# Two more raw tiles by DMA transpose in a mixer and MLP kernel on one core

## The chip, the cores and the metric

The kernel runs on one core of a Trainium2 chip. The metric is the device time of one execution in microseconds (us); the time of a kernel is the median of several runs. The core's engines work side by side and meet at semaphores: TensorE (PE, with its weight loads as PEld) multiplies, VectorE (DVE) makes the statistics, the norms and the sums, ScalarE (ACT) evicts and applies the gelu, GpSimd (POOL) makes the roots, and SyncE (SP) issues nearly all DMAs, in the order of its queue.

## The reference

The input x has 2048 rows of 512, in bf16. What is computed:

```python
h = gelu(layernorm(x) @ w1)                    # w1: 512 x 512
# four column blocks of h, shifted by +1, -1, +2, -2 rows, zeros at the ends
hs = concatenate([g0, g1, g2, g3], axis=-1) @ w2
x1 = x + hs
h2 = gelu(layernorm(x1) @ w3) @ w4             # w3: 512 x 1792, w4: 1792 x 512
return x1 + h2
```

## The kernel before

The rows are cut into 16 tiles of 128 rows; tile t holds the rows 16p + t, so that a shift of the rows by one is the same partition in the next tile, except at the ends. A tile is 128 KB.

The first product, x @ w1, needs each tile with its columns on the partitions (xnT). It is reached in two ways. Tiles 6 to 15 are normed first: statistics (st, L289), their aggregate (ag, L294), the root on POOL (rs, L300), the norm (nm, L309); then they are transposed in pairs, the pairs 8 and 10 on TensorE (tp8, tp10, L323, eight 128x128 transposes each, evicted by ACT as ev8, ev10, L332), the pairs 6, 12 and 14 by a DMA transpose from SBUF (td0_6, td0_12, td0_14, L343). A pair's product is m1p (L410), and ACT writes its gelu (g1p, g1s, L420 and L425) in the transposed layout that the second product wants.

Tiles 0 to 5 are raw: they are transposed as they come from memory, multiplied as they are (m1r, L378), copied out by ACT (rc, L388), and the layernorm is put right afterwards by DVE (zr, L393) with the column sums of w1 (colsum, L366, four matmuls cs0 to cs; their eviction is cse, L370). Tiles 0 to 3 are transposed on TensorE, four transposes each (tp0 to tp3, L323), and evicted by ACT (ev0 to ev3, 128x512). Tiles 4 and 5 come transposed by one DMA straight from DRAM (tdx_4, L351). The raw tiles' gelu (g1r, L399) is transposed by DMA in pairs (th, L357).

Then follow the second product and the sum x1 (m2, L436 and L450; L460 on DVE), the second layernorm with its DMA transposes (td1, L343), and the two big products of the MLP (m3h L492 and m3 L468 with w3, m4 L511 with w4), with their outputs. They begin at tile 8.

The order on each engine is written out by hand in lists of names (firsts, from L634); what is not in a list follows in the order of the code. Every operation waits for what it reads and writes over by semaphores. An engine, and SP with its DMAs, takes its list strictly in order, so an operation that waits holds up all that stand behind it on that engine. Loads are named ldx (a tile of x, L272), ldw1 (L542), ldw2 (L546), ldw3a and ldw3b (L552). Their order on SP before:

```python
firsts["sp"] = """ldx0 ldw11 ldx6 ldw13 ldx7 ldx2 ldx8 ldx3 ldx9 tdx_4 ldx10 ldx11 ldx12 td0_6 ldx13 ldx14 ldx15
    ldw20 ldw21 ldw22 ldw23 td0_12 td0_14 ldw3a0 ldw3a1 ldw3a2 ldw3a3 th_0 td1_8 ldw3b0 ...
```

ACT's queue issues three loads at the start (ldw10, ldw12, ldx1).

Of the kernel before, what the change touches and what calls it, by code (L numbers as in the profile page):

```python
# [171 lines left out]
def bass_standalone__mixer_s_mlp__prompt_kernel(nc: bass.Bass, x, w1, w2, w3, w4, out):  # L172
# [15 lines left out]
    with ExitStack() as es:  # L188
# [82 lines left out]
        def load_x(t, n, eng="sp"):  # L271
            add(eng, f"ldx{t}", lambda e: e.dma_start(x_sb[:, t : t + n, :], xd[:, t : t + n, :]),  # L272
                writes=[(("x", i), 0) for i in range(t, t + n)], dma=True)
# [40 lines left out]
        def tp(t, n, b, raw):  # L314
            src = x_sb if raw else xn
            rd = [(("x", i), 0) if raw else (("xn", i), 0) for i in range(t, t + n)]

            def f(e):
                ins = None
                for i in range(n):  # L320
                    for c in range(DC):
                        o = 1024 * b + (i * DC + c) * P
                        ins = e.transpose(psb[:, o : o + P], src[:, t + i, P * c : P * (c + 1)], ident[:])  # L323
                return ins

            add("pe", f"tp{t}", f, reads=rd + [("ident", 1)], writes=bres(b, 1, f"tp{t}"))

        def ev(t, n, b, eng="act"):
            src = psb[:, 1024 * b : 1024 * b + n * D]
            dst = xnT[:, t : t + n, :, :].rearrange("p t c s -> p (t c s)")  # L330
            if eng == "act":
                f = lambda e: e.activation(dst, src, ACT_F.Copy)  # L332
            else:
                f = lambda e: e.tensor_copy(dst, src)
            add(eng, f"ev{t}", f, reads=bres(b, 1, f"tp{t}"), writes=[(("xT", i), 0) for i in range(t, t + n)])
# [13 lines left out]
        def tdma_x(t):  # L349
            add("sp", f"tdx_{t}",  # L350
                lambda e: e.dma_start(xnT[:, t : t + 2, :, :].rearrange("p t c s -> p (t c) s"),  # L351
                                      xd[:, t : t + 2, :].rearrange("p t d -> p (t d)"), transpose=True),
                writes=[(("xT", i), 0) for i in (t, t + 1)], dma=True)
# [20 lines left out]
        def m1r(t, b, c0=0, c1=DC):  # L374
            def f(e):
                ins = None
                for c in range(c0, c1):
                    ins = e.matmul(bank(b), xnT[:, t, c, :], w1_sb[:, c, :], start=(c == 0), stop=(c == DC - 1))  # L378
                return ins

            rd = [(("xT", t), 0)] + W1[c0:c1]
            if c0:
                rd += bres(b, 1, f"m1r{t}{c0}")
            end = f"{c1}" if c1 < DC else ""
            add("pe", f"m1r{t}{end}", f, reads=rd, writes=bres(b, 1, f"m1r{t}{end}"))

        def rc(t, b):
            add("act", f"rc{t}", lambda e: e.activation(yraw[:, t, :], bank(b), ACT_F.Copy),  # L388
                reads=bres(b, 1, f"m1r{t}"), writes=[(("yraw", t), 0)])
# [168 lines left out]
        load_w1(2, "act")  # L558
        load_w1(3, "sp")
        load_x(1, 1, "act")  # L560
        for t, n in ((6, 1), (7, 1), (2, 1), (8, 1), (3, 1), (9, 1), (10, 1), (11, 1), (12, 1), (13, 1), (14, 1), (15, 1), (4, 2)):
            load_x(t, n)
        for c in range(DC):
            load_w2(c)
# [7 lines left out]
            colsum(4, c)  # L572
        colsum_out(4)
        for t in range(R):
            if t < 4:
                tp(t, 1, 6 + t % 2, True)
                ev(t, 1, 6 + t % 2, "act")
            elif t == 4:
                tdma_x(t)
            cuts = [0, 1, 2, 3, 4] if t == 0 else [0, 2, 4] if t == 1 else [0, 4]  # L580
            for c0, c1 in zip(cuts, cuts[1:]):
                m1r(t, YB[t], c0, c1)
            rc(t, YB[t])
# [39 lines left out]
        for t in (8, 10):  # L623
# [7 lines left out]
            tdma(1, t, 2)  # L631

        firsts = {}
        firsts["pe"] = """wu tp0 cs0 cs1 m1r01 m1r02 tp1 m1r03 cs2 m1r0 cs tp2 m1r12 m1r1 tp3 m1r2 m1r3 m1r4 m1r5 tp8 m1p6  # L634
            tp10 m1p8 m1p10 m2_8a m2_9a m2_8 m2_9b m2_9 m2_10a m2_11a m2_12a m2_13a m1p12 m1p14 m2_10 m2_11
            m2_12b m2_13b m2_14a m2_15a m2_12 m2_13 m2_14b m2_15b m2_14 m2_15""".split()
        firsts["act"] = """ldw10 ldw12 ldx1 table ev0 ev1 rc0 ev2 ev3 rc1 rc2 rc3 rc4 rc5 ev8 cse g1p6 ev10 g1p8 g1s10 g1s11
            g1r0 g1r1 g1p12 g1p14 g2h_0_0_0 g2h_0_0_4 g1r2 g1r3 g2h_0_0_8 g2h_0_0_12 g1r4 g1r5""".split()
        firsts["dve"] = """pada padb padc padd pade padf st0_0 st0_6 st0_7 ag0_6 ag0_7
            st0_8 nm0_6 nm0_7 st0_9 ag0_8 ag0_9 st0_10 st0_11 nm0_8 nm0_9 ag0_10 ag0_11  # L640
            st0_12 nm0_10 nm0_11 st0_13 ag0_12 ag0_13 st0_14 st0_15 ag0_14 ag0_15 nm0_12 nm0_13 st0_1 ag0_0 ag0_1
            nm0_14 nm0_15 zr0 zr1 x1_8 x1_9 st1_8 st1_9 ag1_8 ag1_9 st0_2 nm1_8 nm1_9 st0_3 ag0_2 ag0_3 x1_10 x1_11 st1_10
            st1_11 ag1_10 ag1_11 x1_12 nm1_10 nm1_11 x1_13 x1_14 x1_15 zr2 zr3 st0_4 st0_5 ag0_4 ag0_5 zr4 zr5
            st1_12 st1_13 ag1_12 ag1_13""".split()
        firsts["pool"] = """ident0 ident1 neghalf stz ste rs0_6 rs0_8 rs0_10
            rs0_12 rs0_14 rs0_0 rs1_8 rs0_2 rs1_10""".split()
        firsts["sp"] = """ldx0 ldw11 ldx6 ldw13 ldx7 ldx2 ldx8 ldx3 ldx9 tdx_4 ldx10 ldx11 ldx12 td0_6 ldx13 ldx14 ldx15 ldw20 ldw21 ldw22 ldw23 td0_12 td0_14 ldw3a0 ldw3a1
            ldw3a2 ldw3a3 th_0 td1_8 ldw3b0 ldw3b1 ldw3b2 ldw3b3 ldx4 td1_10 th_2 th_4 td1_12 td1_14 ldw4""".split()

        slots = [4, 0, 2]  # L650
# [111 lines left out]
```

## Time and profile before

| | before |
|---|---|
| median of 3 runs | 136.77 us (136.63 to 137.22) |
| the profiled execution | 136.71 us, of which the span 134.7 us |
| busy: PE, PEld | 131.6 us (98%), 69.7 us |
| busy: DVE, ACT, POOL | 58.2 us, 46.7 us, 12.5 us |
| granted TensorE clock | 1.0 |
| DMA moved | 12.96 MB, HBM read 6.82 MB |

The span runs from the first to the last instruction. Starts in the timeline are us from the span's start. A row of the timeline has the start, the length, the engine (SPq is a DMA's issue on SP, not its transfer), the line in the code, the operation, what it writes and reads, how many were merged, and in brackets how long the engine was idle before it and what ended that. A DMA lands when its last completion has come.

### The profile page before, as it was taken

Reading aid. Unit: us, or ns where it says so; the run is one execution under the profiler, and the core shown is the slowest. Engines: PE = TensorE matmul, PEld = TensorE weight load, DVE = VectorE, ACT = ScalarE, POOL = GpSimd, SP = SyncE. Lnnn points to the kernel's source line nnn. Section 1 sums busy time; section 2 is a strip of 40 time slices with the busy share of each in tenths; the row PEclk is TensorE's granted clock in tenths of the full one; section 3 lists DMA queues with packets and bytes.
Section 4 is the critical chain, followed back from the end, with each engine's and each line's share of the span. In section 5 each row is a group of like instructions: output and inputs, shape, how many; then the busy total and the mean of one; then the engine's idle time right before and its main releaser. Section 6 shows DMA issues by size and latency. Waiting matters only on the chain.

```text
span 134.7 us, 1809 instructions
## 1 busy us (share of the span) xinstructions
PE 131.6 (98%) x729; PEld 69.7 (52%) x729; DVE 58.2 (43%) x135; ACT 46.7 (35%) x56; POOL 12.5 (9%) x25
## 2 busy tenths in 40 slices
PE   7999999999999999999999999999999999999993
PEld 2446867668884444444444444444444444444452
DVE  0689989799967777762222000122200002322222
ACT  3387871507963035550001555200066630000000
POOL 2032422220330012220000000000000000000000
PEclk9999999999999999999999999999999999999999
DMA  3999489984465893444111000011110001111121
GB/s 110 335 230 198 145 160 246 243 276 95 78 124 101 260 298 75 81 80 78 39 61 56 5 0 0 0 39 39 39 39 5 0 0 39 39 39 39 42 76 43
DMA packets 24568, 12.96 MB, mean 96 GB/s; under 512 B 16752, under 2 KB 23920, under 8 KB 24560
## 3 DMA queue, kind: packets, MB, share of 16 engines
q1 hardware_dynamic: 23984, 12.42, 36.4%
q10 hardware_dynamic: 576, 0.43, 1.0%
q8 instruction: 6, 0.10, 0.3%
q14 instruction: 2, 0.02, 0.1%
HBM read 6.82 MB, written 2.10 MB: 66 GB/s over the span
## 4 chain that ended last, share of the span: by engine, by line
PE 98%; DVE 0%; issue 0%
PE ps L511 36%; PE ps L468 27%; PE ps L492 9%; PE ps L410 6%; PE ps L436 5%; PE ps L450 5%; PE ps L378 4%; PE ps L534 2%; PE ps L323 2%; PE ps L366 1%; DVE o_sb L523 0%
## 5 line engine op out<-in xcount | busy, mean ns | idle before, releaser
L511 PE MATMUL ps<-w_sb,h2T 128*128 128x512 bf16 (+2 forms) x238 | 48.9, 366 | 0.0
L523 DVE TENSOR_TENSOR o_sb<-ps,x_sb 128x512 bf16<-128x512 f32 (+2 forms) x17 | 11.2, 660 | 61.2 <-PE ps L511 61.2
L479 ACT ACTIVATE h2T<-ps 128x1024 bf16<-128x1024 f32 x21 | 21.5, 1024 | 46.2 <-PE ps L468 46.2
L468 PE MATMUL ps<-x1nT,w_sb 128*128 128x512 bf16 x168 | 36.8, 379 | 0.0
L511 PEld LDWEIGHTS ps<-w_sb,h2T 128*128 128x128 bf16 x238 | 22.8, 98 | 25.9
L468 PEld LDWEIGHTS ps<-x1nT,w_sb 128*128 128x128 bf16 x168 | 16.4, 98 | 19.8
L289 DVE BATCH_NORM_STATS2 st<-x_sb 128x6 f32<-128x512 bf16 x32 | 20.9, 681 | 3.9 <-DMA x_sb<-in_x_dram 3.9
L300 POOL TENSOR_TENSOR rstd<-mv,neghalf 128x2 f32<-128x2 f32 x16 | 11.6, 725 | 46.2 <-DVE mv L294 46.2
L492 PE MATMUL ps<-x1nT,w_sb 128*128 128x256 bf16 x112 | 12.4, 273 | 0.0
L460 DVE TENSOR_TENSOR x_sb<-ps,x_sb 128x512 bf16<-128x512 f32 x16 | 10.6, 686 | 2.9 <-PE ps L436 1.5
L492 PEld LDWEIGHTS ps<-x1nT,w_sb 128*128 128x128 bf16 x112 | 10.9, 98 | 1.6
L410 PE MATMUL ps<-xnT,w_sb 128*128 128x256 bf16 x80 | 9.2, 273 | 0.0
L503 ACT ACTIVATE h2T<-ps 128x1024 bf16<-128x1024 f32 (+1 forms) x8 | 7.1, 915 | 6.0 <-PE ps L492 6.0
L410 PEld LDWEIGHTS ps<-xnT,w_sb 128*128 128x128 bf16 x80 | 7.7, 98 | 1.2
L309 DVE TENSOR_SCALAR x1n<-x_sb,mv,rstd 128x512 bf16<-128x512 bf16 x16 | 5.9, 411 | 5.3 <-POOL rstd L300 5.3
L450 PE MATMUL ps<-w_sb,hTf 128*128 128x512 bf16 x32 | 7.2, 379 | 0.0
L436 PE MATMUL ps<-w_sb,hTf 128*128 128x512 bf16 x32 | 7.1, 379 | 0.0
L378 PE MATMUL ps<-w_sb,xnT 128*128 128x512 bf16 x24 | 6.4, 399 | 0.0
L420 ACT ACTIVATE hTf<-ps 128x1024 bf16<-128x1024 f32 x4 | 4.1, 1024 | 4.1 <-PE ps L410 4.1
L332 ACT ACTIVATE xnT<-ps 128x512 bf16<-128x512 bf16 (+1 forms) x6 | 4.4, 736 | 2.6 <-PE ps L323 2.6
L294 DVE BATCH_NORM_AGGREGATE mv<-st 128x2 f32<-128x9 f32 x32 | 5.0, 186 | 0.0
L436 PEld LDWEIGHTS ps<-w_sb,hTf 128*128 128x128 bf16 x32 | 3.1, 98 | 3.6
(28 smaller groups left out, 37.1 us busy)
## 6 DMA issues: line engine op xcount, KB each, us to landing
out_dram<-o_sb SPq DMA_DIRECT2D x15, 128.0 KB, 1.8
w_sb<-in_w_dram SPq DMA_DIRECT2D x1, 1792.0 KB, 8.0
x_sb<-in_x_dram SPq DMA_DIRECT2D x13, 128.0 KB, 3.2
w_sb<-in_w_dram SPq DMA_DIRECT2D x4, 256.0 KB, 4.4
w_sb<-in_w_dram SPq DMA_DIRECT2D x6, 128.0 KB, 3.1
w_sb<-in_w_dram SPq DMA_DIRECT2D x4, 192.0 KB, 3.1
w_sb<-in_w_dram ACTq DMA_DIRECT2D x2, 128.0 KB, 3.3
x_sb<-in_x_dram SPq DMA_DIRECT2D x1, 256.0 KB, 3.9
```

The lines of the kernel that those rows point to most:

```text
L289: add("dve", f"st{layer}_{t}", lambda e: e.bn_stats(st9[:, i, 0:6], src[:, t, :]), reads=[(r, 0)], writes=[(("st6", i), 0)])
L300: lambda e: e.tensor_tensor(rstd[:, i : i + n], mv[:, i : i + n, 1], neghalf[:, 0:n], ALU.pow),
L378: ins = e.matmul(bank(b), xnT[:, t, c, :], w1_sb[:, c, :], start=(c == 0), stop=(c == DC - 1))
L410: ins = e.matmul(dst, w1_sb[:, c, P * fc : P * (fc + 1)], xnT[:, t : t + 2, c, :], start=(c == 0), stop=(c == DC - 1))
L436: ins = e.matmul(bank(b), hTf[:, c0 : c0 + P], w2_sb[:, j, :], start=(j == 0), stop=(j == DC - 1))
L450: ins = e.matmul(bank(b), hTf[:, w[0] : w[0] + P], w2_sb[:, j, :], start=first and n == 0, stop=last and n == len(js) - 1)
L460: lambda e: e.tensor_tensor(x1_sb[:, t, :], bank(b), x_sb[:, t, :], ALU.add),
L468: ins = e.matmul(bank(b), w3_sb[:, c, P * fc : P * (fc + 1)], x1nT[:, 4 * q : 4 * q + 4, c, :], start=(c == 0), stop=(c == DC - 1))
L479: lambda e: e.activation(h2T[:, fc : fc + 2, q % 2, :], src, ACT_F.Gelu_apprx_tanh),
L492: ins = e.matmul(dst, w3_sb[:, c, P * (fc + i) : P * (fc + i + 1)], x1nT[:, t : t + 2, c, :], start=(c == 0), stop=(c == DC - 1))
L511: ins = e.matmul(ps[:, 512 * b : 512 * b + c1 - c0], h2T[:, fc, q % 2, P * i : P * (i + 1)], w4_sb[:, fc, c0:c1], start=(fc == 0), stop=(f ...
L523: lambda e: e.tensor_tensor(o_sb[:, k % 4, c0:c1], ps[:, 512 * b : 512 * b + c1 - c0], x1_sb[:, t, c0:c1], ALU.add),
```

## The change

Tiles 2 and 3 are no longer transposed on TensorE: one DMA transpose from DRAM, tdx_2, brings both, as tdx_4 does for 4 and 5. tp2, tp3, ev2 and ev3 go. The plain loads of x2 and x3, which the later sum and the statistics read, become one load of 256 KB that stands behind td0_14 on SP; ldx4 (tiles 4 and 5) keeps its place. On SP tdx_2 stands behind ldx8, and ldw13 has changed places with ldx7. On ACT the eviction of the column sums, cse, moves from behind ev8 to behind rc1. On DVE pair 8 is normed ahead of tile 11's statistics, pair 12 ahead of tile 15's, and tile 2's statistics come behind pair 8's second norm. POOL's list is unchanged.

```diff
-        for t, n in ((6, 1), (7, 1), (2, 1), (8, 1), (3, 1), (9, 1), ..., (15, 1), (4, 2)):
+        for t, n in ((6, 1), (7, 1), (8, 1), (9, 1), ..., (15, 1), (2, 2), (4, 2)):
             load_x(t, n)
...
-            if t < 4:
+            if t < 2:
                 tp(t, 1, 6 + t % 2, True)
                 ev(t, 1, 6 + t % 2, "act")
-            elif t == 4:
+            elif t % 2 == 0:
                 tdma_x(t)
...
-  pe:  ... m1r0 cs tp2 m1r12 m1r1 tp3 m1r2 m1r3 m1r4 m1r5 tp8 m1p6
+  pe:  ... m1r0 cs m1r12 m1r1 m1r2 m1r3 m1r4 m1r5 tp8 m1p6
-  act: ... ev0 ev1 rc0 ev2 ev3 rc1 rc2 rc3 rc4 rc5 ev8 cse g1p6 ev10 ...
+  act: ... ev0 ev1 rc0 rc1 cse rc2 rc3 rc4 rc5 ev8 g1p6 ev10 ...
-  dve: st0_8 nm0_6 nm0_7 st0_9 ag0_8 ag0_9 st0_10 st0_11 nm0_8 nm0_9 ag0_10 ag0_11
-       st0_12 nm0_10 nm0_11 st0_13 ag0_12 ag0_13 st0_14 st0_15 ag0_14 ag0_15 nm0_12 nm0_13 st0_1 ag0_0 ag0_1
-       nm0_14 nm0_15 zr0 zr1 x1_8 x1_9 st1_8 st1_9 ag1_8 ag1_9 st0_2 nm1_8 nm1_9 st0_3 ag0_2 ag0_3 ...
+  dve: st0_8 nm0_6 nm0_7 st0_9 ag0_8 ag0_9 st0_10 nm0_8 nm0_9 st0_11 ag0_10 ag0_11
+       st0_12 nm0_10 nm0_11 st0_13 ag0_12 ag0_13 st0_14 nm0_12 nm0_13 st0_15 ag0_14 ag0_15 st0_1 ag0_0 ag0_1
+       nm0_14 nm0_15 zr0 zr1 x1_8 x1_9 st1_8 st1_9 ag1_8 ag1_9 nm1_8 nm1_9 st0_2 st0_3 ag0_2 ag0_3 ...
-  sp:  ldx0 ldw11 ldx6 ldw13 ldx7 ldx2 ldx8 ldx3 ldx9 tdx_4 ldx10 ldx11 ldx12 td0_6 ... td0_14 ldw3a0
+  sp:  ldx0 ldw11 ldx6 ldx7 ldw13 ldx8 tdx_2 ldx9 tdx_4 ldx10 ldx11 ldx12 td0_6 ... td0_14 ldx2 ldw3a0
```

More of the change, by code (lines that the diff above doesn't have):

```diff
@@ L560, in bass_standalone__mixer_s_mlp__prompt_kernel @@
         load_x(1, 1, "act")
-        for t, n in ((6, 1), (7, 1), (2, 1), (8, 1), (3, 1), (9, 1), (10, 1), (11, 1), (12, 1), (13, 1), (14, 1), (15, 1), (4, 2)):
+        for t, n in ((6, 1), (7, 1), (8, 1), (9, 1), (10, 1), (11, 1), (12, 1), (13, 1), (14, 1), (15, 1), (2, 2), (4, 2)):
             load_x(t, n)
@@ L633, in bass_standalone__mixer_s_mlp__prompt_kernel @@
         firsts = {}
-        firsts["pe"] = """wu tp0 cs0 cs1 m1r01 m1r02 tp1 m1r03 cs2 m1r0 cs tp2 m1r12 m1r1 tp3 m1r2 m1r3 m1r4 m1r5 tp8 m1p6
+        firsts["pe"] = """wu tp0 cs0 cs1 m1r01 m1r02 tp1 m1r03 cs2 m1r0 cs m1r12 m1r1 m1r2 m1r3 m1r4 m1r5 tp8 m1p6
             tp10 m1p8 m1p10 m2_8a m2_9a m2_8 m2_9b m2_9 m2_10a m2_11a m2_12a m2_13a m1p12 m1p14 m2_10 m2_11
             m2_12b m2_13b m2_14a m2_15a m2_12 m2_13 m2_14b m2_15b m2_14 m2_15""".split()
-        firsts["act"] = """ldw10 ldw12 ldx1 table ev0 ev1 rc0 ev2 ev3 rc1 rc2 rc3 rc4 rc5 ev8 cse g1p6 ev10 g1p8 g1s10 g1s11
+        firsts["act"] = """ldw10 ldw12 ldx1 table ev0 ev1 rc0 rc1 cse rc2 rc3 rc4 rc5 ev8 g1p6 ev10 g1p8 g1s10 g1s11
             g1r0 g1r1 g1p12 g1p14 g2h_0_0_0 g2h_0_0_4 g1r2 g1r3 g2h_0_0_8 g2h_0_0_12 g1r4 g1r5""".split()
         firsts["dve"] = """pada padb padc padd pade padf st0_0 st0_6 st0_7 ag0_6 ag0_7
-            st0_8 nm0_6 nm0_7 st0_9 ag0_8 ag0_9 st0_10 st0_11 nm0_8 nm0_9 ag0_10 ag0_11
-            st0_12 nm0_10 nm0_11 st0_13 ag0_12 ag0_13 st0_14 st0_15 ag0_14 ag0_15 nm0_12 nm0_13 st0_1 ag0_0 ag0_1
-            nm0_14 nm0_15 zr0 zr1 x1_8 x1_9 st1_8 st1_9 ag1_8 ag1_9 st0_2 nm1_8 nm1_9 st0_3 ag0_2 ag0_3 x1_10 x1_11 st1_10
+            st0_8 nm0_6 nm0_7 st0_9 ag0_8 ag0_9 st0_10 nm0_8 nm0_9 st0_11 ag0_10 ag0_11
+            st0_12 nm0_10 nm0_11 st0_13 ag0_12 ag0_13 st0_14 nm0_12 nm0_13 st0_15 ag0_14 ag0_15 st0_1 ag0_0 ag0_1
+            nm0_14 nm0_15 zr0 zr1 x1_8 x1_9 st1_8 st1_9 ag1_8 ag1_9 nm1_8 nm1_9 st0_2 st0_3 ag0_2 ag0_3 x1_10 x1_11 st1_10
             st1_11 ag1_10 ag1_11 x1_12 nm1_10 nm1_11 x1_13 x1_14 x1_15 zr2 zr3 st0_4 st0_5 ag0_4 ag0_5 zr4 zr5
@@ L646, in bass_standalone__mixer_s_mlp__prompt_kernel @@
             rs0_12 rs0_14 rs0_0 rs1_8 rs0_2 rs1_10""".split()
-        firsts["sp"] = """ldx0 ldw11 ldx6 ldw13 ldx7 ldx2 ldx8 ldx3 ldx9 tdx_4 ldx10 ldx11 ldx12 td0_6 ldx13 ldx14 ldx15 ldw20 ldw21 ldw22 ldw23 td0_12 td0_14 ldw3a0 ldw3a1
+        firsts["sp"] = """ldx0 ldw11 ldx6 ldx7 ldw13 ldx8 tdx_2 ldx9 tdx_4 ldx10 ldx11 ldx12 td0_6 ldx13 ldx14 ldx15 ldw20 ldw21 ldw22 ldw23 td0_12 td0_14 ldx2 ldw3a0 ldw3a1
             ldw3a2 ldw3a3 th_0 td1_8 ldw3b0 ldw3b1 ldw3b2 ldw3b3 ldx4 td1_10 th_2 th_4 td1_12 td1_14 ldw4""".split()
```

## The prediction, made before the changed kernel was run

> **What bounds the kernel now.** I read the chain that ended last first, then the same chain in order of time, then the timeline of the first 30 us, and last the busy share of the DMA engines there. The page's busy shares and its chain:
>
> ```profile
> PE   7999999999999999999999999999999999999993
> ...
> DMA  3999489984465893444111000011110001111121
> ...
> PE 98%; DVE 0%; issue 0%
> ```
>
> TensorE is the bound from the first microsecond to the last store, so time is won only where TensorE has less to do, and lost wherever it waits. The DMA row has nines in its second to fourth slices (a slice is 3.37 us, so from 3.4 to 13.5 us): there the transfers are as full as TensorE. The chain in order of time, with start and length in us, around the change:
>
> ```profile
> 7.22 0.22 PE ps L323 x4
> 7.44 0.86 PE ps L378 x4
> 8.31 0.22 PE ps L323 x4
> 8.53 3.45 PE ps L378 x16
> 11.98 0.45 PE ps L323 x8
> 12.43 1.75 PE ps L410 x16
> ```
>
> The two x4 rows of L323 are tp2 and tp3, 0.22 us each, and they are what the change removes. The 16 matmuls of L378 are m1r2 to m1r5; the x8 row is tp8; the L410 row is m1p6, which reads what td0_6 brings. The timeline shows how little time is left there:
>
> ```profile
> 5.01 1.39 SPq L351 DMA_TRANSPOSE xnT<-in_x_dram  x1
> ...
> 8.60 1.26 SPq L343 DMA_TRANSPOSE xnT<-xn  x1
> ...
> 9.64 1.29 DVE L289 BATCH_NORM_STATS2 st<-x_sb 128x6 f32<-128x512 bf16 x2 [0.23 <-DMA x_sb<-in_x_dram]
> ...
> 12.21 1.68 PEld L410 LDWEIGHTS ps<-xnT,w_sb 128*128 128x128 bf16 x16
> ```
>
> DVE waits for tile 10 itself (landed 9.62 by the trace). td0_6 is issued at 8.60 and lands at 12.03, and the weight load of m1p6, which reads it, starts at 12.21: 0.18 us of room. Next, the DMA engines; the last two columns are their busy share and GB/s:
>
> ```profile
> 4.50:5.50 1.00, 1.00 1.06 349
> 5.50:6.50 1.00, 1.00 1.00 305
> 6.50:7.50 1.00, 1.00 1.06 216
> 7.50:8.50 1.00, 1.00 1.15 216
> 8.50:9.50 1.00, 1.00 1.03 286
> 9.50:10.00 0.50, 1.00 0.71 204
> 10.00:11.00 1.00, 1.00 1.21 187
> ```
>
> They are full from 4.5 us until td0_6 lands, but for some 0.15 us after 9.5 (0.29 of half a microsecond). A transfer added ahead of td0_6 therefore delays it. The landings, from the trace's completions: x6 5.12, x1 5.30, w1 row block 3 (ldw13) 5.68, x7 6.06, x2 6.40, x8 6.92, x3 7.28, x9 8.15, tdx_4 9.23, x10 9.62, x11 9.97, x12 10.77, td0_6 12.03.
>
> **The change, part by part.**
>
> *TensorE.* It loses tp2 and tp3: 2 x 0.22 = 0.44 us, all on the path. The floor is thus 136.71 - 0.44 = 136.27 us. The Trainium skill ("TensorE: Matmul & The Clock Gate", Part 4: PE-mode transpose) gives about 275 ns for one such 128x128 transpose in a kernel; its eight would be an estimated 2.2 us, but the trace has 0.22 us for four of them, and the measurement decides.
>
> *DMA work ahead of td0_6.* Two loads (x2, x3) go and one transpose from DRAM (tdx_2) comes. A load: five landings from x1 (5.30) to x3 (7.28) take 1.98 us, 0.40 each. The transpose: x3 (7.28) to x11 (9.97) is 2.69 us for tdx_4 and three loads, so 2.69 - 1.20 = 1.50 us. Added work: 1.50 - 0.79 = 0.71 us, less the 0.15 idle, 0.56. So td0_6 lands at about 12.03 + 0.56 = 12.59. Following the queue gives the same: x8 takes x2's place (6.40), tdx_2 7.90, x9 8.30, tdx_4 9.80, x10 10.2, x11 10.6, and td0_6 2.05 behind it as before (9.97 to 12.03), less the 0.15: 12.5 to 12.65. No row shows two such transposes so close. From below, the second could cost the 1.24 us by which td0_14 lands behind td0_12 (19.47, 20.71); from above, the whole 1.95 us from x3 to tdx_4. I take 1.50, the same operation's own row.
>
> *SP's queue.* Ahead of td0_6 it loses two issues of 0.47 us and gains one transpose issue: 1.39 and a slower next issue (0.57 after tdx_4 instead of 0.43), some 1.55 us. It reaches td0_6 at about 7.97 + 1.55 - 0.95 = 8.57, where before it stood waiting from 7.97 for the norm. The norm of pair 6 comes no later: x7 lands in ldw13's place (5.68 for 6.06), and x8, held up before a transpose as x9 was, at some 6.9, when the statistics of tile 8 started anyway (6.95). So td0_6 is issued at 8.6 as before; only its landing moves. ldw13 lands at 6.06; its first reader's weight load was at 6.41, so nothing there.
>
> *The raw tiles on TensorE.* m1r1's first matmul may start at 7.06; its evicted tile is ready at 6.99, so it starts within 0.1 of that. m1r2 then comes at 7.9 and meets tdx_2 (7.9): 0.1. m1r4 comes at 9.75 and meets tdx_4 (9.80): 0.15 to 0.2. Both waits only use up room that the wait for td0_6 would take anyway: m1r5 ends at 11.65, tp8 runs behind the norm of pair 8 (below), and TensorE stands ready for m1p6 at about 12.15.
>
> *m1p6.* The one weight load that shows a wait for a DMA transpose started 0.10 us after the landing (34.40 to 34.51). So m1p6 loads at 12.59 + 0.10 = 12.69 instead of 12.21, **0.48 us later**. Everything behind is TensorE end to end, so this stays to the end.
>
> *DVE's order.* x10 lands at 10.2 instead of 9.62, statistics 10.2 to 10.9, and now pair 8 is normed before tile 11's statistics: 0.59 behind the start of st0_10, so 10.8 to 11.55; before, 10.85 to 11.57. This move pays for x10's delay and no more. Pair 10 pays instead: tile 11's statistics 0.69, two aggregates 0.3, the root 0.70 with its hand-overs: normed at 13.2 to 13.9 instead of 12.54 to 13.28. tp10 was at 14.01 and now comes at 14.49: covered, but a bound if m1p6 were early. Pair 12 ahead of tile 15: DVE waits 0.2 for its root and td0_12 goes at 16.3 instead of 16.14; m1p12 loads at 21.2, td0_12 lands 3.3 after its issue: hidden. Tile 15 and pair 14 follow: td0_14 goes at 18.7 instead of 17.58 and lands at 21.8; m1p14 starts near 23.6: hidden.
>
> *ACT.* Two evictions fewer (0.60 each) and ncs earlier. Every ACT step behind m1p6 hangs on TensorE (g1p6 waits 0.19, g1p8 0.26), so nothing is won or lost.
>
> *x2-3 behind td0_14.* One 256 KB load, 0.69 us by the spacing of the w3 loads of that size (23.73, 24.48, 25.11), lands near 22.9; the statistics of tile 2 now stand behind pair 8's second norm at 24.1: hidden. But it stands ahead of ldw3a, th_0 and td1_8. th_0 landed 5.43 and td1_8 6.34 us behind td0_14; now 21.8 + 5.43 + 0.69 = 27.9 and 28.85. The matmul that first reads th_0 was at 27.72, now 28.20: covered. The first m3h was at 28.36, now 28.84; with the landing at 28.85 and 0.13 to the first matmul (34.40 to 34.54) it could wait 0.14. Its lower end is no wait (td1_8 is issued at 24.2 and its kind landed in 3.0 to 3.3 elsewhere, 27.5); I take none, since 6.34 holds a stretch (21 to 22.5 us) in which the engines moved little for no reason in this change.
>
> *Sum.* -0.44 of work, +0.92 of waiting: **+0.48 us**. 136.71 (span 134.7 and 2.0 around it) + 0.48 = 137.19; the median of three is 136.77, 0.06 above, so 137.2.
>
> **The rivals.**
>
> *The transpose costs no more than the loads it replaces* (20%). The trace has 1.24 as the least spacing and 1.50 against 0.79, which speaks against it; for it speaks that tdx_4's 1.50 was taken in a mixture. Then td0_6 lands by 12.03, m1p6 is bound by it or by tp10 (x10, issued 0.6 later, lands near 10.0, pair 10 normed by 13.7, 0.25 ahead of before): 0.1 to 0.3 won, 136.5. The Trainium skill ("Advanced Engine Details and Errata", X-Bar Transpose (TRN2)) states that transpose DMAs are as fast as regular ones: by that rule this rival holds. The trace speaks against it: 256 KB in 1.50 us, against 0.79 for two loads.
>
> *The transpose costs more* (20%), the other side. Place: DMA engines between x8 and td0_6. The shift is its cost less 1.02 (0.79 for the loads, 0.15 idle, 0.18 of room less the 0.10 from landing to load); at 1.95 us it is 0.93 and the time 137.6. It counts as slower from 1.76 (137.45). For it: x9, issued before tdx_4, came 0.87 behind x3 and not 0.40.
>
> *td1_8 is late too* (12%): 0.14 more, 137.3; up to 0.5 more if the slow stretch grows.
>
> *The change gives what it removes*, 136.27 (3%): it needs x10 and td0_6 no later than now. The forecast has the remaining 45%.
>
> **How the numbers follow.** A measurement tells about 0.5% (0.68 us) from no change. Faster than that lies below the floor of 136.27: 4%, for errors. Slower is above 137.45: the costly transpose and part of the late td1_8 and of the forecast's upper end: 28%. The rest, 68%, is within. The range runs from the cheap transpose, 136.4, to the costly one with some wait at td1_8, 137.9.
>
> **What would show it.** Right: tdx_2 lands near 7.9, tdx_4 near 9.8, x10 near 10.2, td0_6 near 12.6, and the chain has m1p6's first load near 12.7, with TensorE idle some 0.5 before it. Wrong: td0_6 by 12.1, or TensorE waiting at tp8, tp10, th_0's reader or the first m3h instead.

## The result, and the profile after

The changed kernel takes 137.36 us in the median of 14 runs (136.99 to 137.83), the kernel before 136.73 (136.50 to 137.22): 1.0045 times as long, with a 95% interval of 1.0030 to 1.0059, some 0.6 us. Its profiled execution took 137.14 us, its span is 135.04 us against 134.65.

The time is what the prediction said. The place is not. First the chain that ended last, from the page of the kernel after:

```profile
PE 77%; DVE 9%; DMA 6%; SPq 5%; POOL 2%; issue 1%
```

Before it was TensorE from end to end (98%). Now it runs through loads, DVE's statistics and a DMA before it comes to TensorE. In order of time, the pieces (start, length) around the place where it changes over:

```profile
7.25 2.73 DMA x_sb<-in_x_dram
...
18.05 0.40 DVE xn L309
18.46 1.32 DVE zraw L393 x2
19.78 1.20 DVE x_sb L460 x2
20.98 1.19 DVE st L289 x2
22.17 0.24 DVE mv L294 x2
22.41 0.07 issue
22.48 0.70 POOL rstd L300
23.20 0.73 DVE x1n L309 x2
23.97 4.71 DMA x1nT<-x1n
28.68 0.14 issue
28.81 12.39 PE ps L492 x112
```

The change-over is at 28.68 us, where td1_8 lands and the first m3h may start. Up to there it is DVE's chain and DMAs that set the time; from 28.81 on TensorE runs as before. What TensorE waited for, in the kernel after (total, times, longest):

```profile
PEld ps L378 <- DMA xnT<-in_x_dram: 1.0, 1, 1.0
...
PEld ps L492 <- DVE x_sb L460: 0.7, 1, 0.7
...
PEld ps L450 <- DMA hTf<-hraw: 0.5, 1, 0.5
```

These are idle times of the weight loads, which run ahead of the matmuls; what the matmuls lost is less. The first row is m1r2 waiting for tdx_2: 0.66 us lost from start to start. The third is m2_14 waiting for th_0: 0.19 lost. The second is the first m3h; the row names a sum on DVE, but the semaphore that came last is td1_8's landing: 0.36 lost. The timeline of the kernel after has the first wait, and the issues on SP that stand ahead of the others (the row of 16.11 is two issues, td0_12 and td0_14, with the time between them):

```profile
8.24 3.63 PE L378 MATMUL ps<-w_sb,xnT 128*128 128x512 bf16 x16 [0.49 <-DMA xnT<-in_x_dram]
...
8.82 1.24 SPq L343 DMA_TRANSPOSE xnT<-xn  x1
...
12.15 1.91 PE L410 MATMUL ps<-xnT,w_sb 128*128 128x256 bf16 x16
...
16.11 3.60 SPq L343 DMA_TRANSPOSE xnT<-xn  x2
...
19.76 0.58 SPq L272 DMA_DIRECT2D x_sb<-in_x_dram  x1
...
22.29 1.25 SPq L357 DMA_TRANSPOSE hTf<-hraw  x1
...
23.97 2.70 SPq L343 DMA_TRANSPOSE x1nT<-x1n  x1
...
24.80 3.82 PE L450 MATMUL ps<-w_sb,hTf 128*128 128x512 bf16 x16
```

The two waits behind it stand in a timeline of 17 to 30 us; the matmul's own row of the first m3h names td1_8:

```profile
27.79 0.33 PEld L450 LDWEIGHTS ps<-w_sb,hTf 128*128 128x128 bf16 x3 [0.52 <-DMA hTf<-hraw]
...
28.81 1.36 PE L492 MATMUL ps<-x1nT,w_sb 128*128 128x256 bf16 x11 [0.20 <-DMA x1nT<-x1n]
```

In the kernel before, the first m3h starts without a wait:

```profile
28.36 1.80 PE L492 MATMUL ps<-x1nT,w_sb 128*128 128x256 bf16 x15
```

m1p6 (the L410 row) starts at 12.15, and its first weight load at 12.12 against 12.21 before: the kernel after is 0.11 us **ahead** there in this execution, and still is when the L450 row of 24.80 begins. Both waits that cost time come behind it. Starts of matmuls and landings, read from the traces:

| us | before | after |
|---|---|---|
| tdx_2, tdx_4 land | none, 9.23 | 8.20, 9.55 |
| x10, x11 land | 9.62, 9.97 | 9.98, 10.33 |
| td0_6 issued, lands | 8.60, 12.03 | 8.82, 12.08 |
| m1p6 starts | 12.27 | 12.15 |
| td0_14 issued, lands | 17.58, 20.71 | 18.48, 21.89 |
| th_0 lands, its reader m2_14 starts | 26.14, 27.72 | 27.75, 27.79 |
| td1_8 issued, lands | 23.74, 27.05 | 23.97, 28.68 |
| first m3h starts | 28.36 | 28.81 |

-0.11 at m1p6, +0.19 and +0.36 at the two waits, and -0.06 where before waited for td1_10 (34.40): +0.38 by the traces, and the spans differ by 0.39. The medians differ by 0.63; what makes the rest is in no trace.

### The profile page after: what moved, and what is told of

It reads as the page before. It is cut to its first block, busy times and chain, and to the rows that moved or that the text cites. A ratio compares the mean times of both kernels' runs of the same rounds, so it can differ in the third digit from the quotient of the medians.

```text
span 135.0 us, 1792 instructions
## 1 busy us (share of the span) xinstructions
PE 131.1 (97%) x721; PEld 68.6 (51%) x721; DVE 58.2 (43%) x135; ACT 46.0 (34%) x54; POOL 12.4 (9%) x25
## 4 chain that ended last, share of the span: by engine, by line
PE 77%; DVE 9%; DMA 6%; SPq 5%; POOL 2%; issue 1%
PE ps L511 36%; PE ps L468 27%; PE ps L492 9%; PE ps L436 5%; DMA x1nT<-x1n 3%; DVE st L289 3%; SPq L351 2%; DMA x_sb<-in_x_dram 2%; DVE xn L309 2%; SPq L272 2%; POOL rstd L300 2%; DVE zraw L393 1%; DVE x_sb L460 1%; DVE mv L294 1%; SPq L542 1%
## 5 line engine op out<-in xcount | busy, mean ns | idle before, releaser
L460 DVE TENSOR_TENSOR x_sb<-ps,x_sb 128x512 bf16<-128x512 f32 x16 | 10.6, 682 | 2.0 <-PE ps L436 2.0
L410 PE MATMUL ps<-xnT,w_sb 128*128 128x256 bf16 x80 | 9.2, 273 | 0.0
L410 PEld LDWEIGHTS ps<-xnT,w_sb 128*128 128x128 bf16 x80 | 7.6, 98 | 1.2
L450 PE MATMUL ps<-w_sb,hTf 128*128 128x512 bf16 x32 | 7.4, 380 | 0.0
L436 PEld LDWEIGHTS ps<-w_sb,hTf 128*128 128x128 bf16 x32 | 3.1, 98 | 3.6
L450 PEld LDWEIGHTS ps<-w_sb,hTf 128*128 128x128 bf16 x32 | 3.0, 98 | 3.6 <-DMA hTf<-hraw 0.5
```

Source lines behind the costliest of these rows:

```text
L410: ins = e.matmul(dst, w1_sb[:, c, P * fc : P * (fc + 1)], xnT[:, t : t + 2, c, :], start=(c == 0), stop=(c == DC - 1))
L436: ins = e.matmul(bank(b), hTf[:, c0 : c0 + P], w2_sb[:, j, :], start=(j == 0), stop=(j == DC - 1))
L450: ins = e.matmul(bank(b), hTf[:, w[0] : w[0] + P], w2_sb[:, j, :], start=first and n == 0, stop=last and n == len(js) - 1)
L460: lambda e: e.tensor_tensor(x1_sb[:, t, :], bank(b), x_sb[:, t, :], ALU.add),
```

## The experiments

The theory after the result: th_0 and td1_8 come too late, because td0_14 is issued 0.9 us later and the load of tiles 2 and 3 stands behind it. The rival is the mechanism of the forecast: the loss is made ahead of m1p6 by the second DRAM transpose. A third question is why 0.44 us less work on TensorE gives only 0.11. Ratios are to the kernel before on the same chip, with 95% intervals.

**e5_x2_gap: the load moved to a stretch in which SP is idle.**

```diff
-  sp: ... ldw23 td0_12 td0_14 ldx2 ldw3a0 ...
+  sp: ... ldw23 ldx2 td0_12 td0_14 ldw3a0 ...
```

> The changed kernel with one move: the plain load of tiles 2 and 3 stands behind ldw23, ahead of td0_12, where SP and the DMA engines stand idle (13.6 to 16.1 and 15.7 to 17.0 us in the changed kernel). Theory (late transposes): nothing stands ahead of th_0 and td1_8 that did not before, but td0_14 is still 0.9 us later than before; th_0 lands near 27.0, td1_8 near 28.0, at most 0.1 us of waiting for them and none for ldw3b, 136.6 to 136.8 us. Rival (loss made ahead of m1p6): 137.2 to 137.4.

Measured: 136.80 us, 1.0008 (0.9996 to 1.0019), against 1.0045 with the load behind td0_14. One move of one load takes back most of the loss, and nothing ahead of m1p6 was touched by it; m1p6 even starts later in its trace than in that of the kernel after (12.35 for 12.15). th_0 lands at 26.99 and td1_8 at 27.90, and no matmul waits for either. td0_14 was issued later than in the kernel after (18.98 for 18.48) and td1_8 landed 0.77 earlier all the same, though single landings vary by as much (see e2).

**e2_pair12_old: DVE's order for pair 12 as before, the load where the change put it.**

```diff
-  dve: ... st0_14 nm0_12 nm0_13 st0_15 ag0_14 ag0_15 st0_1 ...
+  dve: ... st0_14 st0_15 ag0_14 ag0_15 nm0_12 nm0_13 st0_1 ...
```

> The changed kernel with before's order for pair 12: tile 15's statistics ahead of its norm. Theory (late transposes): pair 14's norm ends 0.45 us earlier, td0_14 is issued near 18.0 instead of 18.5, th_0 lands near 27.3, td1_8 near 28.2; at most 0.1 us of waiting is left, 136.6 to 136.8 us. If the 256 KB load alone makes the loss: 137.3. Rival (the loss is made ahead of m1p6): 137.2 to 137.4.

Measured: 136.88 us, 1.0012 (0.9996 to 1.0027). This edit alone, too, takes back most. td0_14 was issued at 18.20 instead of 18.48, th_0 landed at 27.02 and td1_8 at 27.95, without a wait. The issue moved by 0.28 us, less than the expected 0.45; the rest of the 0.9 stays, since pair 12 is late already (td0_12 issued at 16.75, 16.14 before). The landing moved by 0.73, which the order does not explain, but one trace does not tell this finely: e6 and e9, described below, have the same program from td0_12 to td1_8 and land td1_8 at 27.87 and 27.08. The medians carry this result, not the trace. That either edit is nearly enough fits a bound with little room: TensorE wants td1_8 some 0.1 ahead of 28.3, and only both together push it past.

**e6_x2_gap_p12: both edits.**

> The same, and before's order for pair 12 as well. Theory (late transposes): td1_8 near 27.6, no wait there; m1p6 starts at 12.1 to 12.3 as in all the kernels so far, so 136.5 to 136.7 us: no more than 0.2 us below before, because the 0.44 us of transposes are spent waiting for tdx_2, tdx_4 and td0_6. Rival (loss made ahead of m1p6): 137.2 to 137.4.

Measured: 136.66 us, 0.9999 (0.9987 to 1.0011): as before, with 0.44 us less to do. m1p6 started at 12.09, the first m3h at 28.27. th_0 landed at 26.93 and td1_8 at 27.87, both in time. td1_8's issue on SP is shorter than above:

```profile
21.66 1.25 SPq L357 DMA_TRANSPOSE hTf<-hraw  x1
...
23.66 2.15 SPq L343 DMA_TRANSPOSE x1nT<-x1n  x1
...
28.27 1.91 PE L492 MATMUL ps<-x1nT,w_sb 128*128 128x256 bf16 x16
```

**e4_before_plus: the kernel before with 512 KB more behind td0_14.**

```diff
+            xdup = sb("xdup", [P, 4, D], BF16)
+            add("sp", "ldxd", lambda e: e.dma_start(xdup[:, 0:4, :], xd[:, 2:6, :]), ...
-  sp: ... td0_14 ldw3a0 ...
+  sp: ... td0_14 ldxd ldw3a0 ...
```

> The kernel before with one DMA more behind td0_14, 512 KB of x into a buffer that nothing reads (twice the load that the change puts there); nothing else is changed. Theory (late transposes): two loads of 0.69 us ahead of th_0 and td1_8 bring them to 27.5 and 28.45; TensorE wants td1_8 by 28.25, so 0.1 to 0.5 us lost, 136.9 to 137.2 us. Rival (the loss is made ahead of m1p6): this stage has room, 136.7 us as before.

Measured: 137.39 us, 1.0043 (1.0028 to 1.0059), above the expected range: the same loss as that of the change, in a kernel that has neither tdx_2 nor the new order on DVE. The profiled execution took 136.83 us (the runs 136.83 to 137.96): td1_8 landed at 28.36 and the first m3h lost 0.19, the only wait behind m1p6. The rest of the median's loss is in no trace. With e5 this points to the place: the stage between td0_14 and the first m3h has room for less than 512 KB.

**e1_x2_late and e3_both: a bad place for the load.**

```diff
-  sp: ... td0_14 ldx2 ldw3a0 ... th_0 td1_8 ldw3b0 ...
+  sp: ... td0_14 ldw3a0 ... th_0 td1_8 ldx2 ldw3b0 ...
-  dve: ... nm1_8 nm1_9 st0_2 st0_3 ag0_2 ag0_3 x1_10 ... x1_15 zr2 zr3 ...
+  dve: ... nm1_8 nm1_9 x1_10 ... x1_15 st0_2 st0_3 ag0_2 ag0_3 zr2 zr3 ...
-  act: ... g2h_0_0_4 g1r2 g1r3 g2h_0_0_8 g2h_0_0_12 ...
+  act: ... g2h_0_0_4 g2h_0_0_8 g2h_0_0_12 g1r2 g1r3 ...
```

> The changed kernel with the plain load of tiles 2 and 3 behind td1_8 on SP, ahead of ldw3b (their statistics, POOL's root and the two gelus move back with it). Theory (late transposes: in the changed kernel TensorE is 0.11 us ahead of before until it waits 0.19 us for th_0 and 0.36 us for td1_8, because 256 KB more and a td0_14 issued 0.9 us later stand ahead of them): th_0 lands near 27.1 and td1_8 near 28.0, no wait for either, first m3h at 28.25, about 136.6 us, 0.15 below before. Rival (the forecast on record: the loss is made ahead of m1p6 by the second DRAM transpose): stays at 137.2 to 137.4.

> Both edits together: the load of tiles 2 and 3 behind td1_8, and before's order for pair 12. Theory (late transposes): td1_8 lands near 27.5, no wait, and nothing is won over the late load alone, since TensorE is then bound by its waits for tdx_2 and td0_6: 136.5 to 136.6 us. Rival (the loss is made ahead of m1p6): 137.2 to 137.4.

Measured: 137.16 us, 1.0031 (1.0015 to 1.0047), and 136.95 us, 1.0022 (1.0009 to 1.0035). Both expectations missed the total. In e1 the first m3h did start early, at 28.42 (td1_8 at 28.28), but the load had only moved its delay on: ldw3b's last part landed at 32.67 instead of 31.53, and the m3h that reads it lost 0.90:

```profile
31.80 0.27 PE L492 MATMUL ps<-x1nT,w_sb 128*128 128x256 bf16 x1
...
32.80 0.38 PE L492 MATMUL ps<-x1nT,w_sb 128*128 128x256 bf16 x2 [0.73 <-DVE mv L294]
```

The row names DVE's aggregate, which was long done; the landing at 32.67 is what came just before. This execution took 137.65 us, 0.49 more than e1's median, so the median loses less than the trace shows. In e3 that part was in time (31.70), and 0.26 was lost at 43.47, in the second product behind a sum on DVE; its cause stays open. As tests of the theory the two are poor, since they add waits of their own.

**e9_no_tdx_wait and e10_no_tdx2: where the 0.44 us went.** e9 is e6 with

```diff
-                    ins = e.matmul(bank(b), xnT[:, t, c, :], w1_sb[:, c, :], ...
+                    ins = e.matmul(bank(b), xnT[:, t % 2, c, :], w1_sb[:, c, :], ...
```

and e10 leaves tdx_2 out as well.

> e6_x2_gap_p12 with the raw products m1r2 to m1r5 reading the transposed tiles 0 and 1 in place of 2 to 5 (the products of tiles 2 to 5 are thus of other rows); both DRAM transposes are still issued. TensorE no longer waits for them. Theory (several bounds stand close behind one another ahead of m1p6): TensorE comes early to tp8 and waits there for pair 8's norm (11.5), then for td0_6 (near 12.0); m1p6 at 12.0 to 12.1, 136.5 to 136.7 us, no more than 0.15 below e6. Rival (the wait for tdx_2 alone eats the 0.44 us): 136.2 to 136.3 us.

> The same, and tdx_2 is left out altogether (its DMA work and its issue on SP are gone, nobody reads what it would bring). What a second transpose costs, all in: x10 lands near 9.2, pair 8 is normed near 10.9, td0_6 is issued as soon as pair 6 is normed (8.5) and lands near 11.8; m1p6 near 11.9, 136.3 us, 0.3 to 0.4 below e6. If DMA work is not what holds this stage: as e9.

Measured: e9 136.64 us, 0.9997 (0.9985 to 1.0008); e10 135.99 us, 0.9948 (0.9928 to 0.9967). e9's timeline ahead of m1p6:

```profile
6.83 4.48 PE L378 MATMUL ps<-w_sb,xnT 128*128 128x512 bf16 x20
...
11.45 0.62 PE L323 MATMUL ps<-ident,xn 128*128 128x128 bf16 x8
...
12.19 1.64 PEld L410 LDWEIGHTS ps<-xnT,w_sb 128*128 128x128 bf16 x16 [0.29 <-DMA xnT<-xn]
```

The raw products run through (20 matmuls in 4.48), TensorE is early, and loses 0.30 at tp8, which waits for pair 8's norm, and 0.29 at m1p6, which waits for td0_6. Taking the first wait away wins nothing, since two more stand close behind it. The traces of the changed kernel and of the experiments that share its program up to there show the same: what TensorE has gained is lost each time, but at a different place, in e1 by a late start (m1r1 at 7.43). An empty cell is no loss.

| lost by TensorE, us | after | e1 | e2 | e3 | e5 | e6 |
|---|---|---|---|---|---|---|
| m1r2, for tdx_2 | 0.66 | | 0.45 | 0.32 | 0.11 | 0.62 |
| m1r4, for tdx_4 | | | | 0.10 | 0.59 | |
| tp8, for pair 8's norm | | | | 0.16 | | |
| m1p6, for td0_6 | | 0.03 | 0.26 | | | |
| tp10, for pair 10's norm | | | | 0.17 | 0.17 | 0.09 |
| m1p6 starts at | 12.15 | 12.22 | 12.29 | 12.12 | 12.35 | 12.09 |

The kernel before started m1p6 at 12.27, and e4, with before's program up to there, at 12.21. So the 0.11 of lead in the kernel after is one execution's figure and no gain to count on. In e10's timeline tp8 and m1p6 follow without a wait:

```profile
8.67 1.24 SPq L343 DMA_TRANSPOSE xnT<-xn  x1
...
11.36 0.61 PE L323 MATMUL ps<-ident,xn 128*128 128x128 bf16 x8
...
11.81 1.91 PE L410 MATMUL ps<-xnT,w_sb 128*128 128x256 bf16 x16
```

There x10 lands at 8.69 (10.04 in e9) and x12 at 9.36 (11.10). So the second transpose's DMA work and its place on SP cost 0.65 us of the kernel's time by the medians (136.64 to 135.99) and 0.39 by the two profiled spans: about as much as the 0.44 us of TensorE work that it replaces, by the medians more than that and than the 0.3 to 0.4 expected.

**e8_before_tdup: such a transpose added to the kernel before.**

```diff
+            tdup = sb("tdup", [P, 2, DC, P], BF16)
+            add("sp", "tdup", lambda e: e.dma_start(tdup..., xd[:, 2:4, :]..., transpose=True), ...
-  sp: ... ldx8 ldx3 ldx9 tdx_4 ...
+  sp: ... ldx8 tdup ldx3 ldx9 tdx_4 ...
```

> The kernel before with one DMA transpose from DRAM more (tiles 2 and 3 into a buffer that nothing reads) behind ldx8 on SP, and nothing taken away: the cost of such a transpose by itself. By the 1.50 us on record: td0_6 lands near 13.4, m1p6 starts near 13.5, 1.2 us lost, 137.9 us. By 1.0 to 1.25 us, as the profile of the changed kernel has it (x8 to x11 in 3.15 us with two loads between): td0_6 near 13.0, 0.8 us lost, 137.5 us.

Measured: 138.19 us, 1.0103 (1.0084 to 1.0121), above both expectations; m1p6 starts at 13.53. The start is the first of the two expected, but not by its path: td0_6 landed at 12.80, not 13.4, and TensorE lost 1.15 at tp3, which waits for x3, now behind the added transpose:

```profile
9.13 0.40 PE L324 MATMUL ps<-ident,x_sb 128*128 128x128 bf16 x4 [0.99 <-DMA x_sb<-in_x_dram]
```

The cost of one is read from the landings: x2 6.84 to x11 11.43 is 4.59 us for five loads and two transposes, so with 0.40 for a load 1.30 each.

**e7_x12_late: e6 with ldx12 behind td0_6.**

```diff
-  sp: ... ldx11 ldx12 td0_6 ldx13 ...
+  sp: ... ldx11 td0_6 ldx12 ldx13 ...
```

> The same as the one before, and ldx12 behind td0_6 on SP. Theory: td0_6 is issued as soon as pair 6 is normed and lands near 11.7; m1p6 is then bound by tp8 (pair 8's norm) and tp10 by pair 10's norm; 136.4 to 136.7 us. If td0_6 is not what holds m1p6 but tdx_2 and tdx_4 are: no change to the one before.

Measured: 136.60 us, 0.9991 (0.9981 to 1.0001). The best that computes the whole, but its interval reaches past 1: not shown to be faster than before. In its profiled execution pair 6 was normed late, td0_6 was issued at 8.93 and landed at 12.15, so it does not show what was expected of it.

## Why the prediction was right in its time and wrong in its place

*TensorE's 0.44 us.* Right as work: in e10, where no matmul waits behind the start, the span is 0.51 us shorter than before's (134.14 for 134.65): the 0.44 and the 0.06 that before lost at td1_10. TensorE came to m1r1 at 7.04 there and at 7.28 before, tp2's 0.22 apart, so an early start does not make it. The medians differ by 0.73, of which the profile shows no more than that.

*Cost of the DRAM transpose.* Mis-sized: forecast as 1.50; 1.25 in the kernel after (ldw13 at 6.24 to x11 at 10.33, four loads of 0.40 and two transposes), 1.30 in e8, and 1.35 by x10's landing in e9 and e10. x10 and x11 came at 9.98 and 10.33 instead of 10.2 and 10.6, tdx_4 at 9.55 instead of 9.80, but tdx_2 at 8.20 instead of 7.90, since x8 ahead of it came at 7.18, where the sum had 6.40; x10 was thus 0.36 later than before, and pair 8 normed in time as worked out (11.34, expected 11.55). The rule of the Trainium skill that the prediction quotes ("Advanced Engine Details and Errata", X-Bar Transpose (TRN2)), that transpose DMAs are as fast as regular ones, would make it 0.79: no run here has it that low, though it was nearer than 1.95.

*td0_6 "2.05 behind x11 as before".* This step failed. It landed 1.75 behind x11, at 12.08 and not 12.59. The 2.05 of before was mostly the transpose's own time from its issue and not a queue: in e10 it was issued with x12 about to land and an idle stretch ahead, and still took 3.03 us. It took 3.43 before and 3.38 in e4, without the second transpose, and 3.16 to 3.62 in the nine traces with it. The row for this was there: the forecast itself had td0_12 landing 3.3 us behind its issue, with nothing else under way (it was issued at 16.14, and ldw23 had landed at 16.03). A landing that is set by its own issue does not move when work is put ahead of it, as long as that work is done by then: x12, the last of it, landed at 11.01.

*m1p6 0.48 later.* So this failed as well: 0.11 earlier, and no later than 12.35 in any trace with the changed kernel's start, where 12.27 + 0.48 = 12.75 was due. The wait at m1r2 was 0.66 and not 0.1, since TensorE was there at 7.59 instead of 7.9 and tdx_2 at 8.20. Both signs that the prediction named as showing it wrong came: td0_6 by 12.1, and waits at th_0's reader and the first m3h.

*td0_14, th_0, td1_8.* The landings were right: expected 21.8, 27.9 and 28.85, measured 21.89, 27.75 and 28.68. But the forecast held them against a TensorE that was to be 0.48 late, and found th_0 covered and td1_8 short by 0.14, which it then left out. Against a TensorE 0.11 early the same landings cost 0.19 and 0.36. The same 0.6 us was counted as lost ahead of m1p6, where it was not, and left uncounted at the two waits, where it was. The time is set by the later of TensorE and the landing; that the forecast put both at nearly the same moment (28.84 and 28.85) is luck, and it kept the sum right with the first of them wrong. The landing was partly luck too: from td0_14's landing to td1_8's, the forecast took 6.34 us without the load, and the other traces with no load between have 4.76 (e10) to 6.36 (e8). The rival "td1_8 is late too" had the mechanism, at 12%; it put the wait at 0.14, up to 0.5 more, and named no wait for th_0, where the two cost 0.55.

*The rivals.* That the transpose costs no more than the loads fell (e10, e8); that it costs 1.95 fell too. What the change removes was not to be had in any kernel here that carries tdx_2: even with the later loss repaired, m1p6 starts at 12.09 in e6 and 12.19 in e9, where 0.44 less than before would be 11.83.

What stays open: why td1_8's landing differs by 0.8 us between traces with the same program in that stage (e6, e9), what part of the change's loss the later issue of td0_14 has beside the load, and why the runs of the kernel after spread by 0.8 us where those of e7 spread by 0.5.

## What to carry to other kernels

Work taken off the busiest engine was worth nothing here, since the transfers that feed it were as full and the replacement added to them: price the transfer that replaces it in the same stage (here 1.25 to 1.35 us of DMA work for the 0.80 of the loads that went, to save 0.44). Before a delay in the queue is added to a landing, look whether the landing follows the queue or its own issue (td0_6 came 3.0 to 3.6 us behind its issue in every trace). A landing is compared with the time at which its reader wants it, so a shift forecast upstream must not be counted as room downstream unless it is certain: work out both. When a load has to go somewhere, look for a stretch in which its queue is idle and the DMA engines run empty (in the kernel after, SP from 13.6 to 16.1 us, the engines from 16.2 to 17.0) before putting it in front of anything that someone waits for.

## What the runs showed of the hardware

The issue of a DMA transpose on SP is not always its 1.24 us. td1_8's issue took 2.70 us in the kernel after, 2.12 to 2.60 in e1 to e4 and e6, 1.34 to 1.42 before and in e5 and e7 to e9, and 1.66 in e10. It ended 0.03 to 0.10 us ahead of the landing of the last ldw3a, two transfers ahead of it in the queue, in eleven of the twelve traces (26.67 and 26.74 in the kernel after; 0.25 in e10). Why is not shown. It holds up all that stands behind it on SP: ldw3b's first part was issued at 26.71 instead of 25.12.

Two transposes of the same size can be bound differently. td0_6 lands 3.0 to 3.6 us behind its own issue in all twelve traces. td1_8 lands 3.3 to 4.7 us behind its issue, but 0.91 to 1.02 behind th_0, the transfer ahead of it: it follows the queue.

TensorE's start differs from run to run with the same program ahead of it. The 512-column matmuls follow one another every 0.43 us at first and every 0.22 later; the slow pace ends near 6.1 us in the trace of before and near 6.5 in e7's, but by 4.0 in that of the kernel after, which came to m1r1 0.56 us earlier (6.72 for 7.28), only 0.22 of it for the tp2 that is gone. The granted clock stands at 1.00 throughout in the profiles. The Trainium skill ("TensorE: Matmul & The Clock Gate", Part 1: The HAM clock gate) says that the window which releases the clock runs freely, so that the release varies by ±500 ns; these three traces lie some 2.5 us apart. Where a wait stands behind, as at m1r2, the difference is lost again.
